# Sliding-window attention and a hardswish MLP on one core: batch 1 in 64x64 tiles, first-product units moved ahead of its steps, a token ring of six blocks

## Chip, core and metric

The kernel runs on one core of a Trainium2 chip. The metric is the device time of one execution in microseconds (us); less is better. The core has five engines that matter here, each with its own instruction queue: TensorE (PE, with its weight loads as PEld), VectorE (DVE), ScalarE (ACT), GpSimd (POOL) and SyncE (SP). DMA transfers are issued by SP and POOL and are carried out by 16 DMA engines.

## The reference

```python
def _attn_ref(q, k, v):                      # (8, 8, 576, 64) each
    scores = np.matmul(q, k.transpose(0, 1, 3, 2)) / np.sqrt(D)
    rel = pos[:, None] - pos[None, :]
    scores = np.where((rel >= 0) & (rel < 64), scores, -1e9)
    ... softmax over keys
    return np.matmul(attn, v)

def _moe_ref(x, w_in, w_out):                # x (4608, 512), w_in (512, 2048), w_out (2048, 512)
    h = x @ w_in
    g = h * np.clip(h + 3.0, 0.0, 6.0) / 6.0
    return g @ w_out
```

Attention runs over 8 batches of 8 heads, 576 positions and 64 dimensions; each query sees itself and the 63 keys before it. The heads of a token stand side by side in x, so x has 8 x 576 = 4608 rows of 512. The MLP takes x to 2048 and back to 512, with a hardswish between. Inputs and output are float32; the kernel's tiles are bf16.

## The kernel before

**Tiles and stages.** Attention goes in 32 steps t = 4b + g, one for each batch b and pair of heads g. The MLP goes in 9 blocks kb of 512 tokens. A block has 16 first-product units (`hT`, L467 to L471: four matmuls of 128x512 over the 512 rows of w_in), each followed by ACT's relu (L473) and DVE's min and multiply (L474) into `gT`, and 16 second-product units (`acc`, L491 to L495: four matmuls each), of which every fourth closes an output tile that ACT copies (L498) and SP stores (L500). x is kept transposed in `xT`, a ring of XR = 5 x 512 tokens (L57), which a step writes at the place of its batch modulo XR.

**Two forms of a step.** Batches 0 and 1 use the early form. q and k are loaded as 96 partitions of 6 rows (`load_early_qk`, L98), turned with 24 transposes (`t_k`, `t_q`, L221), and copied to `KT` by DVE (L239) and to `QZ` by ACT or DVE (L231). `s0_` (L244) adds the mask by a matmul of `ident` with `outside` ahead of each score matmul (L248, L251), 18 matmuls in all, so that exp (L259, L265) gives the masked weights at once. `pv_early` (L353) has 20 matmuls with the row sum as a 65th column, and `x_early` (L374) turns the result with 5 transposes on PE and a copy into `xT`.

Batches 2 to 7 use 64x64 tiles. q and k come in one tile of 2 x 64 partitions of 9 rows (`load_qk`, L117). `turn` (L276) makes 36 transposes into two PSUM banks, and `turned` (L283) copies them, keys by DVE and queries by ACT. `s_first` and `s_rest` (L296, L310) make 36 score matmuls without a mask, the first four into spare columns of the banks of `turn`. `weights` (L316) takes exp on ACT (L319, L322) and multiplies by the masks `first` and `band` on POOL (L327, L330). `pv` has 48 matmuls (L403). `pv_out` (L412 to L422) sums, inverts and multiplies on DVE, and `x_` (L429) sends the result into `xT` with DMA transposes on SP (L436): one for the big part (`opl`) and one for the first 64 tokens (`opg` in the profile), or four and one where the batch runs over the end of the ring.

V of a batch lies twice in memory: as loaded (`Vn`, or `Un` for 64x64 tiles) and shifted by 64 tokens (`Vs` or `Us`). The shifted copy is made by DVE and ACT for batch 0, and by two or more DMAs on SP otherwise (`shift_early` L149 and L150, `shift` L155 and L156). `Un` and `Us` need columns of ones beside the values (`pads`, L140 and L141). The tiles of batch b share the memory of batch b - 2.

**PSUM.** `ps_o` has one buffer of two banks, `ps_t` three of one, `ps_h` two and `ps_acc` one. A first-product unit of block 0 uses `ps_h`, and for fc 2, 5, 8 and 11 the buffer of `ps_o` (L462).

**Order.** There is no scheduler: each engine's queue has the order in which the program issues. `queue_block(kb)` (L509) puts the 16 first-product units of a block into `moe`, mixed evenly with what is left of the block before's second-product units, and `weave(n)` (L524) issues the next n. L619 to L649 load and set up, L652 to L680 run batch 0, L705 to L745 batch 1, between units of block 0. From t = 7 on `group(t, n)` (L682) issues pv(t), turn(t + 2), the scores of t + 1, pv_out(t), the key copy, x_(t), two units, the query copy and n - 2 units. From step 12 on a step has 8 units.

The loads of q, k, V and the weights are issued by POOL in program order (L620 to L640 for the start). In the start the queue holds batch 0, w_in in three parts, q and k of batch 1's first two pairs, its V in five pieces, q and k of its other two pairs, and w_out in two parts.

Of the kernel before, what the change touches and what calls it, by code (L numbers as in the profile page):

```python
# [20 lines left out]
BIG = 3.0e38  # L21
# [4 lines left out]
D = 64  # L26
# [10 lines left out]
def kernel(  # L37
# [19 lines left out]
    XR = 5 * TB  # L57
# [40 lines left out]
    def load_early_qk(b, pairs, first=0):  # L98
        if first:
            tiles = staged[b]  # L100
        else:
            both = stage.tile([SP, 2, H, R * D], BF16, name="qk6", tag="qk")
            tiles = [both[:, 0], both[:, 1]]
        h = 2 * first
        for n in pairs:
            for t, src in zip(tiles, (q, k)):
                nc.gpsimd.dma_start(  # L107
                    out=t[:, h : h + 2 * n, :],
                    in_=src[b, h : h + 2 * n].rearrange("h (p r) d -> p h (r d)", r=R),
# [4 lines left out]
    def load_qk(b):  # L114
        t = stage.tile([P, H, RL * D], BF16, name="qk9", tag="qk")
        for z, src in enumerate((k, q)):
            nc.gpsimd.dma_start(out=t[halves[z]], in_=src[b].rearrange("h (p r) d -> p h (r d)", r=RL))  # L117
        return t

    def load_early_v(b):  # L120
        vn = Vn[b % 2]
        for m in range(NM):
            n = min(P, S - m * P)
            nc.gpsimd.dma_start(  # L124
                out=vn[:n, m, :, 0:D],
                in_=v[b, :, m * P : m * P + n, :].rearrange("h s d -> s h d"),
# [11 lines left out]
    def pads(b):  # L138
        for t in (Un[b % 2], Us[b % 2]):
            nc.gpsimd.memset(t[:, :, :, 0:VO], 1.0)  # L140
            nc.gpsimd.memset(t[:, :, :, VO + P : VW], 1.0)  # L141

    def shift_early(b, blocks=(0, NM), heads=(0, H), move=nc.sync.dma_start):

        vn, vs = Vn[b % 2], Vs[b % 2]
        hs = slice(*heads)
        m0, m1 = blocks
        m2 = min(m1, NM - 1)
        move(out=vs[W:P, m0:m1, hs], in_=vn[0:W, m0:m1, hs])  # L149
        move(out=vs[0:W, m0 + 1 : m2 + 1, hs], in_=vn[W:P, m0:m2, hs])  # L150
# [32 lines left out]
    def window(t, inside, fill):  # L183

        nc.gpsimd.memset(t[:], inside)
        for sign, base in ((-1, -1), (1, W)):
            nc.gpsimd.affine_select(
                out=t[:], in_=t[:], pattern=[[sign, W]], compare_op=ISGE,
                fill=fill, base=base, channel_multiplier=-sign,
# [9 lines left out]
    def late_windows():  # L199

        for t in (band, first):
            nc.gpsimd.memset(t[:], 1.0)
# [24 lines left out]
    def t_q(t):  # L227
        b, g = divmod(t, NG)
        tp = transposed_heads(ps_t if b else ps_h, staged[b][0], g)
# [86 lines left out]
    def weights(t, s, ss):  # L316
# [3 lines left out]
        for h in range(2):  # L320
# [48 lines left out]
    def x_early(t):  # L369
# [7 lines left out]
        x0 = b * S % XR  # L377
        n = min(S, XR - x0)
        for to, i, j in ((x0, 0, n), (0, n, S)):
            if i < j:  # L380
# [414 lines left out]
```

## Time and profile before

| what | value |
|---|---|
| runs | 336.97, 334.5, 332.69 us; median 334.5 |
| profiled execution | 335.91 us, span 334.2 us |
| mean granted PE clock | 0.989 |
| PE busy | 312.8 us (94%), 4592 matmuls |
| ACT busy | 190.2 us (57%) |
| DVE busy | 173.7 us (52%) |
| POOL busy | 116.5 us (35%) |
| first products on PE (L468) | 143.9 us |
| second products on PE (L492) | 145.3 us |
| POOL's mask products (L330, L327) | 54.2 us and 15.9 us |
| HBM read, written | 36.70 MB, 9.44 MB |

The page gives the busy time of each engine, the span in 40 slices (a digit is the busy share in tenths; PEclk is the clock that PE was granted), the DMA queues, the chain of work that ended last, the costliest groups of instructions, and the DMA issues with their time to landing. Busy times of different engines overlap. The trace behind the page can be asked for the waits of an engine, for a timeline of it, in which square brackets give the idle time before an instruction and what ended it, and for the busy times of chosen stretches. In timelines several instructions of one line are drawn together (x24), with their starts and modelled ends, so neighbours overlap by their pipelining; the distance from start to start is what an instruction costs its engine.

### The profile page before, as it was taken

To read this page: it belongs to the slowest core of one execution; us is meant where nothing else is said; L and a number is where in the kernel's file an instruction comes from. 1 tells how busy PE (TensorE), PEld (TensorE's weight loads), DVE (VectorE), ACT (ScalarE), POOL (GpSimd) and SP (SyncE) were. 2 spreads that over 40 slices of the span, in tenths; PEclk is the share of its full clock that TensorE was granted. 3 is DMA by queue.
4 is the path that set the end of the run, shared out by engine and by line. 5 is a ranking of instruction groups with operands and counts; after the bars stand their busy time and mean duration, and the time that the engine had idled before them with its cause. 6 is when DMAs were issued, how large, how long until landed. Compare 5 with 4: busy or idle time off the path is not lost.

```text
span 334.2 us, 10639 instructions
## 1 busy us (share of the span) xinstructions
PE 312.8 (94%) x4592; PEld 160.4 (48%) x4592; DVE 173.7 (52%) x356; ACT 190.2 (57%) x345; POOL 116.5 (35%) x154
## 2 busy tenths in 40 slices
PE   6979599999799999999899999999999999999992
PEld 2744365454555555555455555555544444444440
DVE  7676357447655555555455555555554543334300
ACT  2868583457676666666566666666664444454320
POOL 8934612136566335633554356333330000000000
PEclk9999889999999999999999999999999999999997
DMA  6999999932339943993499329931111100001011
GB/s 89 165 210 179 231 209 192 199 93 62 92 74 193 118 113 60 187 113 111 79 175 124 115 55 189 121 113 55 52 51 49 65 31 31 33 31 64 32 68 69
DMA packets 59015, 35.86 MB, mean 107 GB/s; under 512 B 40528, under 2 KB 52880, under 8 KB 58960
## 3 DMA queue, kind: packets, MB, share of 16 engines
q0 software_dynamic: 36752, 18.35, 44.2%
q1 hardware_dynamic: 22208, 16.75, 19.5%
q8 instruction: 38, 0.62, 0.7%
q14 instruction: 17, 0.14, 0.1%
HBM read 36.70 MB, written 9.44 MB: 138 GB/s over the span
## 4 chain that ended last, share of the span: by engine, by line
PE 81%; DMA 8%; POOL 5%; ACT 2%; DVE 1%; SPq 1%; issue 1%; POOLq 0%; ACTq 0%
PE acc L492 36%; PE hT L468 34%; DMA qk<-in_q_dram 4%; PE o L403 3%; DMA qk<-in_k_dram 3%; PE s L310 2%; POOL qk L107 1%; PE tk L276 1%; POOL V L124 1%; DVE gT L474 1%; ACT t L473 1%; SPq L436 1%; DMA xT<-opg 1%; PE tq L276 1%; POOL Pz L330 1%
## 5 line engine op out<-in xcount | busy, mean ns | idle before, releaser
L474 DVE SCALAR_TENSOR_TENSOR gT<-t,hT 128x512 bf16<-128x512 bf16 x140 | 96.3, 688 | 126.9 <-ACT t L473 126.8
L473 ACT ACTIVATE t<-hT,half_const 128x512 bf16<-128x512 f32 x140 | 96.2, 687 | 93.0 <-PE hT L468 91.8
L468 PE MATMUL hT<-xT,win 128*128 128x512 bf16 x560 | 143.9, 381 | 4.6 <-DMA xT<-opg 1.7
L492 PE MATMUL acc<-wout,gT 128*128 128x512 bf16 x576 | 145.3, 379 | 0.2 <-DVE gT L474 0.2
L468 PEld LDWEIGHTS <-win 128*128 128x128 bf16 x576 | 55.8, 98 | 68.0 <-issue 3.7
L492 PEld LDWEIGHTS <-gT 128*128 128x128 bf16 x576 | 54.4, 98 | 65.1 <-issue 2.3
L330 POOL TENSOR_TENSOR Pz<-e,band 128x512 bf16<-128x512 bf16 x48 | 54.2, 1145 | 0.0
L327 POOL TENSOR_TENSOR P<-e,first 64x256 bf16<-64x256 bf16 x24 | 15.9, 661 | 103.5 <-ACT e L319 103.5
L498 ACT COPY osb<-acc 128x512 f32<-128x512 f32 x36 | 21.1, 585 | 21.3 <-PE acc L492 20.9
L322 ACT ACTIVATE e<-s 128x512 bf16<-128x512 f32 x48 | 25.7, 590 | 0.0
L283 DVE COPY KT<-tk 128x576 bf16<-128x576 bf16 x24 | 17.7, 739 | 0.6 <-PE tq L276 0.6
L422 DVE TENSOR_TENSOR opl<-o,recs 128x256 bf16<-128x256 f32 x48 | 17.7, 405 | 0.0
L403 PEld LDWEIGHTS <-Pz 64*64 64x64 bf16 x960 | 11.3, 108 | 10.4 <-issue 9.3
L283 ACT COPY QZ<-tq 128x576 bf16<-128x576 bf16 x24 | 15.2, 632 | 0.6 <-PE tq L276 0.6
L133 POOL DMA_DIRECT2D V<-in_v_dram x18 | 14.4, 815 | 0.0
L403 PE MATMUL o<-V,Pz 64*64 64x65 bf16 x960 | 14.1, 195 | 0.1
L231 ACT COPY QZ<-tp 64x576 bf16<-64x576 bf16 x12 | 7.6, 631 | 10.6 <-PE tp L221 10.6
L276 PE MATMUL tq<-ident,qk 64*64 64x64 bf16 x432 | 12.3, 195 | 0.5 <-DVE gT L474 0.5
L276 PE MATMUL tk<-ident,qk 64*64 64x64 bf16 x432 | 12.4, 195 | 0.0
L310 PE MATMUL s<-QZ,KT 64*64 64x64 bf16 x768 | 12.3, 195 | 0.0
L221 PE MATMUL tp<-ident,qk 96*64 96x96 bf16 x192 | 5.6, 208 | 6.0 <-DMA qk<-in_k_dram 6.0
L276 PEld LDWEIGHTS <-qk 64*64 64x64 bf16 x864 | 10.4, 105 | 1.5 <-issue 1.4
(84 smaller groups left out, 227.0 us busy)
## 6 DMA issues: line engine op xcount, KB each, us to landing
out_dram<-osb SPq DMA_DIRECT2D x36, 256.0 KB, 2.2
qk<-in_k_dram POOLq DMA_DIRECT2D x6, 576.0 KB, 6.4
qk<-in_q_dram POOLq DMA_DIRECT2D x6, 576.0 KB, 10.0
V<-in_v_dram POOLq DMA_DIRECT2D x12, 256.0 KB, 6.1
V<-V SPq DMA_DIRECT2D x6, 432.0 KB, 4.5
wout<-in_moe_w_out_dram POOLq DMA_DIRECT2D x2, 1024.0 KB, 17.3
V<-in_v_dram POOLq DMA_DIRECT2D x8, 128.0 KB, 10.2
win<-in_moe_w_in_dram POOLq DMA_DIRECT2D x2, 512.0 KB, 8.0
```

Of the source, the lines that this page charges most:

```text
L276: nc.tensor.transpose(out=hosts[t][z][halves[h], r * W : (r + 1) * W], in_=staged[b][halves[z], 2 * g + h, r * D : (r + 1) * D], identity= ...
L283: (nc.scalar.copy if z else nc.vector.tensor_copy)(out=(QZ[t % 4][:, 0] if z else KT[t % 4][:, W:]).rearrange("q (p r) -> q p r", r=RL), i ...
L310: nc.tensor.matmul(ss[h][halves[i], c, m, r], lhsT=keys(t, h, W * (w - 1), r), rhs=QZ[t % 4][halves[h], 0, w * W : (w + 1) * W], start=Tru ...
L322: nc.scalar.activation(out=e[:].rearrange("p c m r w -> p (c m r w)"), in_=ss[h][:].rearrange("p c m r w -> p (c m r w)"), func=EXP, scale ...
L330: nc.gpsimd.tensor_tensor(out=Pw[t % 4][:, h].rearrange("p c m r w -> p (c m) (r w)"), in0=e[:].rearrange("p c m r w -> p (c m) (r w)"), i ...
L403: nc.tensor.matmul(o[halves[c], i, c0 : c0 + D + 1], lhsT=p, rhs=vt[:, 2 * g + h, v0 : v0 + D + 1], start=(r == 0), stop=(r == 1), skip_gr ...
L422: nc.vector.tensor_tensor(out=opg[:, :, i], in0=ov[:, i, 2:6, 1 : D + 1].rearrange("p (m h) d -> p m h d", h=2), in1=rec[:, i, 2:6].rearra ...
L468: nc.tensor.matmul(hT, lhsT=win16[:, g, fc * P : (fc + 1) * P], rhs=xT[:, g, t0 : t0 + TB], start=(g == 0), stop=(g == NG - 1),)
L473: nc.scalar.activation(out=t1[:], in_=hT, func=RELU, bias=half_const[:], scale=1.0 / 6.0)
L474: nc.vector.scalar_tensor_tensor(out=gT[:, fc, :], in0=t1[:], scalar=1.0, in1=hT, op0=MIN, op1=MULT)
L492: nc.tensor.matmul(acc[:], lhsT=gT[:, fc, ts * P : (ts + 1) * P], rhs=wout16[:, fc, :], start=(fc == 0), stop=(fc == NFC - 1),)
L498: nc.scalar.copy(out=osb[:], in_=acc[:])
```

## The change

Batch 1 (t = 4 to 7) is done in the 64x64 form, and the code for the early form is cut to batch 0. The parts:

- The ring holds 6 blocks of 512 tokens. Then batch 5 (tokens 2880 to 3456) is the one that runs over its end, at 3072. `x_` now splits the big part into at most two transposes at a multiple of 128 tokens.
- q and k of batch 1 are loaded by `load_qk` in two halves of two pairs, its V by `load_v` in three pieces, and its shifted V by `shift(1)`, two DMAs on SP right behind the issues of V.
- The mask tiles are made at the start (`late_windows`), ahead of the loads of batch 1. The memsets of `ident`, `outside`, `band`, `first` and the pads of batch 1 go to DVE; that of `recs` goes later.
- In steps 5 to 7 two of the three mask products, `P0` and the one of the second head, go to DVE (`both`); step 4 has all three on POOL.
- x of steps 4 and 5 goes by DMA transposes, that of 6 and 7 by PE transposes and an ACT copy (`x_turned`).
- The first three units of block 0 are split: three of their four matmuls are issued ahead of `x_early(3)` and the fourth behind it (`begin`), in place of two warm-up matmuls.
- The order of steps 4 to 8 is written out anew, with more units of block 0 before each of them and fewer second-product units between; the order from pv(12) on is as before. The loads of batches 2 and 3 and the shifts of V move with it: q, k and V of batch 2 stand on POOL behind the mask products of step 7, those of batch 3 behind step 8's.
- The PSUM pools of block 0's units are dealt out anew (`ps_acc`, `ps_t` and `ps_o` for single units), and second products of block 0 use `ps_acc` alone.

```diff
-    XR = 5 * TB
+    XR = 6 * TB
...
-    def load_qk(b):
-        t = stage.tile([P, H, RL * D], BF16, name="qk9", tag="qk")
+    def load_qk(b, n=NG, first=0):
+        t = staged[b] if first else stage.tile([P, H, RL * D], BF16, name="qk9", tag="qk")
+        hs = slice(2 * first, 2 * (first + n))
...
-    def weights(t, s, ss):
+    def weights(t, s, ss, muls=(nc.gpsimd,) * 3):
...
-                nc.gpsimd.tensor_tensor(
+                muls[2].tensor_tensor(
                     out=P0[t % 4][:], in0=e0[:], in1=first[0:D].unsqueeze(1).to_broadcast([D, 2, 2, W]), op=MULT
...
-            nc.gpsimd.tensor_tensor(
+            muls[h].tensor_tensor(
                 out=Pw[t % 4][:, h].rearrange("p c m r w -> p (c m) (r w)"),
...
-        edge = (XR - W - x0 % XR) if x0 % XR < XR < x0 % XR + S else NM * P
-        m1 = min(edge // P, NM - 1)
+        m1 = min(NM - 1, (XR - W - x0 % XR) // P)
...
+        for i, j in ((0, m1), (m1, NM - 1)):
+            if i < j:
+                to_x(x0 + W + i * P, flat[:, i:j].rearrange("p m c -> p (m c)"), P, j - i)
...
+    def x_turned(t):
+        b, g = divmod(t, NG)
+        opg, opg0 = opgs.pop(t)
+        tp = ps_t.tile([P, S], BF16, name="xp", tag="bk")
+        nc.tensor.transpose(out=tp[:, 0:W], in_=opg0[:].rearrange("p h d -> p (h d)"), identity=ident[0:D, 0:D])
+        for m in range(NM - 1):
+            nc.tensor.transpose(
+                out=tp[:, W + m * P : W + (m + 1) * P],
+                in_=opg[:, m // 2, m % 2].rearrange("p h d -> p (h d)"), identity=ident[:],
+            )
+        nc.scalar.copy(out=xT[:, g, b * S : b * S + S], in_=tp[:])
...
-            if kb == 0 and fc % 3 == 2 and fc < spare[0]:
-                hT = ps_o.tile([P, 2, 512], F32, name="hTo", tag="o")[:, 0]
+            if part < 2 and fc in halfway:
+                hT = halfway.pop(fc)
             else:
-                pool = ps_t if late[0] == 1 or late[0] and fc % 2 else ps_h
+                if pool is None:
+                    if late[0] == 0:
+                        pool = (ps_h, ps_h, ps_o)[fc - 3] if fc < 6 else ps_t if fc % 2 else ps_acc
+                    else:
+                        pool = ps_t if late[0] == 1 or fc % 2 else ps_h
...
-            for g in range(NG):
+            for g in ((0, 1, 2), (3,), range(NG))[part]:
...
-                    pool = ps_t if (late[0] == 2 or kb == 0) and ts % 2 else ps_acc
+                    pool = ps_t if late[0] == 2 and ts % 2 else ps_acc
...
+    def begin(kb, pools, between):
+
+        for fc, pool in enumerate(pools):
+            moe.popleft()
+            units[kb](fc, 0, pool)
+        between()
+        for fc in range(len(pools)):
+            units[kb](fc, 1)
...
-    staged[1] = load_early_qk(1, pairs=(2,))
-    load_early_v(1)
-    load_early_qk(1, pairs=(NG - 2,), first=2)
+    late_windows()
+    staged[1] = load_qk(1, 2)
+    load_v(1)
+    shift(1)
+    load_qk(1, 2, 2)
...
-    warm(ps_acc, 2)
-    x_early(3)
-
+    queue_block(0)
+    begin(0, (ps_acc, ps_t, ps_t), lambda: x_early(3))
...
-    queue_block(0)
-    weave(6)
-    t_k(NG)
-    t_q(NG)
+    both = (nc.gpsimd, nc.vector, nc.vector)
+    n = NG
+    weave(4)
+    turn_two(n)
     weave(1)
-    for g in range(1, NG):
-        t_k(NG + g)
-        t_q(NG + g)
-        weave(1)
-        s0_(NG + g - 1)
-        weave(1)
-    shift_early(1, blocks=(0, 3))
-    shift_early(1, blocks=(3, NM))
+    turn_two(n + 1)
+    front(n, n + 1)
+    weave(1)
+    front(n + 1, n + 1, both)
+    weave(1)
+    pv(n)
+    pv_out(n)
+    x_(n)
+    weave(1)
+    turn_two(n + 2)
+    pv(n + 1)
+    pv_out(n + 1)
+    x_(n + 1)
+    weave(1)
+    turn_two(n + 3)
+    front(n + 2, n + 3, both)
+    weave(1)
+    front(n + 3, n + 3, both)
+    weave(1)
+    pads(2, nc.gpsimd.memset)
     staged[2] = load_qk(2)
-    pads(2)
     load_v(2)
+    pv(n + 2)
+    pv_out(n + 2)
+    weave(1)
+    pv(n + 3)
+    pv_out(n + 3)
+    x_turned(n + 2)
+    weave(len(moe))
+    late[0] = 1
+    queue_block(1)
+    weave(1)
+    x_turned(n + 3)
     shift(2)
-    late_windows()
+    weave(9)
+    turn_two(2 * NG)
+    weave(2)
+    group(2 * NG - 1, 2)
     staged[3] = load_qk(3)
...
+    pads(3, nc.gpsimd.memset)
     load_v(3)
```

`turn_two(t)` is `turn(t)` and both copies of `turned`; `front(t, host, muls)` is the scores and `weights` of step t.

More of the change, by code (lines that the diff above doesn't have):

```diff
@@ L95, with load_early_qk @@
     halves = (slice(0, D), slice(D, P))
-    def load_early_qk(b, pairs, first=0):
+    def load_early_qk(pairs, first=0):
         if first:
-            tiles = staged[b]
+            tiles = staged[0]
         else:
@@ L136, in load_v, with pads, shift_early @@
             )
-    def pads(b):
+    def pads(b, memset):
         for t in (Un[b % 2], Us[b % 2]):
[L140 to L150, printed above, removed]
+            memset(t[:, :, :, 0:VO], 1.0)
+            memset(t[:, :, :, VO + P : VW], 1.0)
+    def shift_early(g, move):
+        vn, vs = Vn[0], Vs[0]
+        hs = slice(2 * g, 2 * g + 2)
+        move(out=vs[W:P, :, hs], in_=vn[0:W, :, hs])
+        move(out=vs[0:W, 1:NM, hs], in_=vn[W:P, 0 : NM - 1, hs])
     def shift(b):
@@ L476, in unit @@
             )
+        units[kb] = unit
         return [lambda fc=fc: unit(fc) for fc in range(NFC)]
```

106 lines of the change are left out of this document (42 added, 64 removed).

## The prediction

> **What bounds the kernel now.** I read the page's busy line and slices first.
>
> ```profile
> PE 312.8 (94%) x4592; PEld 160.4 (48%) x4592; DVE 173.7 (52%) x356; ACT 190.2 (57%) x345; POOL 116.5 (35%) x154
> ...
> PE   6979599999799999999899999999999999999992
> ...
> PEclk9999889999999999999999999999999999999997
> DMA  6999999932339943993499329931111100001011
> ```
>
> TensorE bounds it nearly everywhere. A slice is 8.36 us: PE is short of 9 in slices 1, 3, 5 and 11 and a little in slice 20; its clock dips in slices 5 and 6, where the DMA engines are full. So only the first 93 us and one later place have anything but matmul work to lose. Next PE's waits, from 14 to 45 us and then from 100 us on:
>
> ```profile
> PE tp L221 <- DMA qk<-in_k_dram: 4.3, 2, 3.7
> ```
>
> ```profile
> PE hT L468 <- DMA xT<-opg: 1.7, 1, 1.7
> ```
>
> The first is the load of batch 1's q and k. The timeline of PE shows where it bites, and a wait of another kind, a VectorE one after the scores of step 9:
>
> ```profile
> 38.87 0.70 PE L221 MATMUL tp<-ident,qk 96*64 96x96 bf16 x24 [3.74 <-DMA qk<-in_k_dram]
> ...
> 69.56 0.81 PE L468 MATMUL hT<-xT,win 128*128 128x512 bf16 x3 [0.76 <-DVE gT L474]
> ```
>
> After the idle time comes a stretch at half clock (columns: PE, PEld, DVE, ACT, POOL busy, clock, DMA share, GB/s):
>
> ```profile
> 36.67:40.09 3.42, 1.22 (x27) 0.87 (x28) 1.07 (x2) 0.47 (x1) 2.28 (x9) 1.00 1.15 265
> 40.09:43.50 3.41, 3.41 (x24) 2.43 (x22) 0.72 (x2) 2.84 (x6) 0.00 (x0) 0.50 1.24 214
> ```
>
> A unit (4 matmuls of 128x512) takes .864 at full clock, so 3.41 us at .50 lose 1.7. The 1.66 us wait in slice 20 is block 4 waiting for the last x transpose; SyncE's timeline shows why:
>
> ```profile
> 155.28 5.57 SPq L436 DMA_TRANSPOSE xT<-opl  x4
> 160.89 1.82 SPq L436 DMA_TRANSPOSE xT<-opg  x1
> ...
> 163.44 1.24 SPq L436 DMA_TRANSPOSE xT<-opl  x1
> 164.73 1.21 SPq L436 DMA_TRANSPOSE xT<-opg  x1
> ```
>
> Batch 4 (tokens 2304 to 2880) runs over the ring's end at 2560: five transposes a step instead of two.
>
> **The stretch that changes** runs from 22.59 us (after x_early(2)) to 93.39 (the start of pv(12)): 70.8 us. Both orders have done 48 units by then, and what follows is the same except for the ring and one queue. PE's waits there are .37, .54, 3.74, .49 (turn 8), .76, .34, .19, .33, .79, .79, with 1.7 lost to the clock: 10.0 in all, so 60.8 is work.
>
> **Work removed.** An early step costs PE, by start to start in its timeline: 24 transposes .63, 18 score and mask matmuls 1.0, 20 pv matmuls .44, 5 transposes .28: 2.35. A step in 64x64 tiles costs 36 transposes .31, 36 score matmuls .42, 48 pv matmuls .41: 1.14. Four steps save 4.8; the turned x of steps 6 and 7 gives back 2 x .28 = .6, and two warm matmuls (.6) go: 4.8 net.
>
> **What the new order waits for first** is the shifted V of batch 1, which pv(4) needs. V's pieces keep their place behind q and k of the first two pairs and their bytes. These are the last V piece, issued at 22.03, and the last piece of the shift before, issued at 35.30 (columns: size, us to landing):
>
> ```profile
> V<-in_v_dram POOLq DMA_DIRECT2D x1, 64.0 KB, 12.7
> ```
>
> ```profile
> V<-V SPq DMA_DIRECT2D x1, 72.0 KB, 6.5
> ```
>
> So V lands at 34.7 and the shift at 41.8. Two early memsets leave POOL (.22 and .17, L621, L185): I take .3 off. The affine selects (1.9 us) move ahead of the batch 1 loads, at nothing: POOL idles there 4.42 for the DMA queue; without that cover +1.9. SyncE's two issues (.58, .59) now wait for V, with nothing queued behind them before x(4). So Us is there at 34.5 + 6.7 = 41.2. Bounds: the 432 KB shifts took 6.8 loaded (issued at 61.8) and 4.0 unloaded (84.6): 38.5 to 41.4. I take the loaded one: slices 4 and 5 are full.
>
> PE reaches pv(4) earlier. The split of the first three units costs 0: warm .6 and the .37 wait leave, xp moves behind three quarters, and unit 2 still ends near 26.8 because x of pair 2 needs its copy. Then three last quarters .65, seven units 6.05, turns 4 and 5 .62, scores 4 and 5 .84, changes of tile size .6 and short bank waits .9: 36.5. It idles 4.7 us, and the half clock follows: from 41.2 to 43.5, losing 1.15.
>
> The Trainium skill, "TensorE: Matmul & The Clock Gate", Part 1 (The HAM clock gate), says the clock falls after at least one idle window of about 3.4 us. The row above differs: 2.2 us idle in a window with 1.22 busy was enough. By the page a 4.7 us idle need not hold a whole window, and the sum would be 1.15 less.
>
> **From 41.2 to pv(12)**: 38 units 32.8; 8 turns 2.5; 7 scores 2.9; 8 pv 3.3; 2 x .3 turned x; 12 changes of tile size at .1: 43.3, so 84.5. To this come waits:
> - clock 1.15 (0 to 1.7).
> - Keys 6 and 7: between hT10 and scores 7 VectorE has two gT (.69), two K copies (.74) and a pv_out (1.35: L412 to L422 at 75.40 to 76.75): 4.2, behind ACT's t .69 and hand-offs: 5.4 to 5.7 against 3.2 of PE work: 2.5 (0 to 2.9).
> - pv(7) needs the one ps_o buffer back: gT and pv_out of 6, 2.0, against one unit: 1.2 (0 to 1.4).
> - pv(8) needs step 8's masks from POOL: 3.3 from scores to the last product at step 9 (68.8 to 72.1), against two units, 1.8: 1.5 (0 to 1.6).
> - pv(9): its masks queue on POOL behind qk 3 (2 x .70), pads (4 x .2) and V 3:
>
> ```profile
> 106.06 2.41 POOL L133 DMA_DIRECT2D V<-in_v_dram  x3
> ```
>
>  4.4 + 2.9 of products against 5.7 of PE: 1.6 (0 to 2.5).
> - Turned x of 7 .24, turn 9 .25, banks .9: 1.4 (.5 to 2).
>
> Together 9.35: pv(12) at 93.85 against 93.39: +.45. Six of the twelve mask products of batch 1 (three of 64x256, three of 128x512) move to VectorE behind the scores of steps 5 to 7, two a step. No row has them: the bounds are .30 (a copy of 64x576, L150) and POOL's .66 and 1.145; I take .4, as L422 (128x256, two inputs), and nothing on the path: they stand behind ACT's exponentials (.27, .26, .59, .59, L319 and L322), and pv comes a unit or more later.
>
> q, k and V of batch 2 are now issued behind POOL's product of step 7, by my sum at 52 to 53, where they went at 45 and 57 before. With .8 of pads ahead, .70 an issue and 9.5 to landing (the q load issued at 97 to 99) q is there at 63; turn 8 comes 16 units after pv(4)'s start, near 64: no wait, 0 to 2 if the cover of 1 us is gone. V 2 lands near 63 and its shift 4.0 later, before pv(8) near 69. The memsets given to VectorE (band, first, pads: about 1.3) run before 22 us while loads are awaited; uncovered they cost up to 1.3.
>
> **After pv(12).** x(11) stands on SyncE behind shift(3), which now waits for V 3 (issued late by POOL): block 2 waits +.7 (0 to 2). The ring of six blocks (3072) ends inside batch 5, which wraps with three transposes instead of five, 3.7 us a step: block 4's stall goes, -1.75 (1.66 plus the restart); next late is the ordinary 2.4 of two transposes, inside 8.17 us a step.
>
> Sum: +.45 + .7 - 1.75 = -.6. The profiled execution took 335.91 (span 334.2), 1.4 above the median of 334.5; 335.9 - .6 - 1.4 = 333.9 for the median.
>
> **The rivals.**
> A, the forecast: work saved 4.8 and the old waits (10) are paid back by an equal set of new ones: 333.9, alone 331.5 to 336.5. Chance .47.
>
> B, the shift lands as if unloaded, by 38.5: idle 2 instead of 4.7, no clock loss: -2.7 - 1.15: 330.0. For: SyncE's queue is not POOL's, and wout's 2 MB are issued after it. Against: all four shift pieces of before took 6.5 to 6.7 in this place. Chance .2; with the waits at pv(7) to pv(9) also at their low ends (-4.3) it is 325.7, a third of it.
>
> C, slower: the shift takes its time by bytes. Before it went in pieces of 216 and 72 KB at 6.5 to 6.7; as 432 KB behind a full queue it could take twice 6.7: Us at 48, PE idle 11.5, a second half-clock window: +6.8 + 1.7: 342.4. From Us at about 42 it ends slower than before, from 46.8 by over 2%. Against: 432 KB took 6.8 at 61.8. Chance .1.
>
> D, VectorE's products are dear: at POOL's prices the six take 5.4 instead of 2.4, in the chain that already ends last at keys 7 and pv(7): +3.0: 336.9. Against: VectorE's two-input rows run at .405 for 256 columns. Chance .13. The Trainium skill, "GPSIMD Engine Reference", section 1 (Specifications), says that GpSimd shares its SBUF interfaces with VectorE and contends with VectorE instructions of two SBUF inputs, which these are; no run of before has the pair.
>
> E, the ring does not do what it says: three transposes a step still let SyncE fall behind and the wait moves to block 5: +1.75: 335.7. Against: 3.7 in 8.17 leaves room where 7.4 did not. Chance .1.
>
> **How the numbers follow.** 2% is 6.7 us, about what a measurement of this kernel can tell from no change. Under 327.8: a third of B and the tail of A's low waits, .1. Over 341.2: C and a tail of D, .12. Between: .78. The range 329.0 to 339.0 holds A, two thirds of B, D and E, and leaves out C and B's low end. Predicted: 333.9.
>
> **What would show it.** Right: pv(4) waits 4 to 5 us for V<-V and starts near 41; one window at .50 follows; scores 7 wait for KT, pv(8) and pv(9) for POOL; pv(12) starts at 93 to 95; no wait for xT in block 4. Wrong: pv(4) before 39 or after 43; VectorE products over .7; waits behind pv(4) under 5 us in all; hT of block 2 waiting over 2 us for xT.

## The result and the profile after

The changed kernel takes 336.56 us (median of 20 runs, 334.96 to 338.35) where the kernel before takes 334.62 us (20 runs, 332.4 to 338.35): 1.0066 of its time, 95% interval 1.004 to 1.0092. It is slower by about 2 us. The forecast was 333.9, a little faster. The profiled execution of the changed kernel took 338.35 us, the longest of the 20 runs, with a span of 336.6 us; no other of the 20 has a lower mean granted clock than its 0.974, and the highest is 0.998. So what is read from this trace on the clock is the upper end of what the change costs there.

The page of the changed kernel, the lines that answer to those shown first:

```profile
PE 308.8 (92%) x4770; PEld 157.8 (47%) x4812; DVE 175.9 (52%) x376; ACT 188.8 (56%) x347; POOL 120.4 (36%) x154
...
PE   6987367988999999999999999999999999999992
...
PEclk9799878999999999999999999999999999999997
DMA  7999992939937932993299429941111110001011
```

PE is busy 4 us less: work went away as meant. But slices 4 to 7 (a slice is 8.4 us), where PE had 9, 5, 9, 9 before, now have 7, 3, 6, 7, and the clock dips in slices 5 to 7 and in slice 2. The dip in slice 2 left no delay that can be seen: pv(3) starts at 21.75 us, before at 21.70. The slice of the old block 4 stall (20) is full. So the loss lies in front of 60 us and the gain behind 93 us. PE's waits from 22 to 100 us:

```profile
PE o L393 <- DMA V<-V: 4.0, 1, 4.0
PE tk L292 <- DVE KT L279: 3.5, 2, 2.1
PE o L393 <- POOL Pz L326: 2.6, 4, 0.9
PE o L393 <- DVE opl L412: 1.9, 1, 1.9
PE hT L472 <- ACT xT L373: 1.0, 2, 0.7
```

They stand in order of size: the shifted V ahead of pv(4), the copies of keys ahead of scores 4 and 6, POOL's mask products ahead of pv(8) and pv(9), and the results of step 6 ahead of pv(7). The three longest in the timeline of PE (lines of three narrow stretches):

```profile
41.56 0.91 PE L393 MATMUL o<-V,Pz 64*64 64x65 bf16 x30 [4.04 <-DMA V<-V]
...
49.63 0.20 PE L292 MATMUL tk<-QZ,KT 64*64 64x64 bf16 x1 [2.12 <-DVE KT L279]
...
57.36 0.45 PE L393 MATMUL o<-V,Pz 64*64 64x65 bf16 x32 [1.93 <-DVE opl L412]
```

The stretch from 22.6 us to the start of pv(12), first in the kernel before, then in the changed kernel (PE, PEld, DVE, ACT, POOL busy, clock, DMA share, GB/s):

```profile
22.60:93.39 70.79, 62.35 (x1058) 34.71 (x1056) 39.82 (x76) 44.19 (x83) 28.26 (x46) 0.98 1.04 158
```

```profile
22.60:98.22 75.62, 59.57 (x1265) 31.22 (x1277) 42.32 (x90) 43.11 (x85) 31.69 (x42) 0.93 1.01 150
```

With half of the busy time at clock .50 counted as loss, the 70.8 us before are 60.6 of work, 8.4 idle and 1.7 lost to the clock; the 75.6 us after are 55.8 of work, 16.1 idle and 3.7 lost to the clock. The work saved is 4.8. Idle time grew by 7.6 and the clock's loss by 2.0. (The page after has 4770 matmuls beside 4812 weight loads, so some matmul records are missing, and idle time is rather too high than too low.) From the start of pv(12) to the end of the span it is 240.8 before and 238.4 after. So: +4.8 up to pv(12), -2.4 behind it, +2.4 in the span.

### The profile page after: what moved, and what is told of

It reads as the page before. It is cut to its first block, busy times and chain, and to the rows that moved or that the text cites. A ratio compares the mean times of both kernels' runs of the same rounds, so it can differ in the third digit from the quotient of the medians.

```text
span 336.6 us, 11066 instructions
## 1 busy us (share of the span) xinstructions
PE 308.8 (92%) x4770; PEld 157.8 (47%) x4812; DVE 175.9 (52%) x376; ACT 188.8 (56%) x347; POOL 120.4 (36%) x154
## 4 chain that ended last, share of the span: by engine, by line
PE 78%; DMA 7%; POOL 7%; DVE 2%; issue 2%; ACT 2%; SPq 0%; POOLq 0%; ACTq 0%
PE acc L500 36%; PE hT L472 33%; DMA V<-in_v_dram 5%; PE o L393 4%; PE s L306 2%; DMA V<-V 2%; PE tk L272 1%; POOL qk L107 1%; POOL V L126 1%; POOL Pz L326 1%; ACT t L480 1%; PE tq L272 1%; DVE gT L481 1%; POOL V L134 1%; POOL win L160 1%
## 5 line engine op out<-in xcount | busy, mean ns | idle before, releaser
L472 PE MATMUL hT<-xT,win 128*128 128x512 bf16 x561 | 147.3, 382 | 2.3 <-ACT xT L373 1.0
L472 PEld LDWEIGHTS <-win 128*128 128x128 bf16 x576 | 55.8, 99 | 67.6 <-issue 3.0
L500 PEld LDWEIGHTS <-gT 128*128 128x128 bf16 x576 | 54.2, 98 | 63.2 <-issue 0.6
L326 POOL TENSOR_TENSOR Pz<-e,band 128x512 bf16<-128x512 bf16 x53 | 60.2, 1154 | 13.6 <-ACT e L318 13.6
L318 ACT ACTIVATE e<-s 128x512 bf16<-128x512 f32 x56 | 30.0, 588 | 0.7 <-PE s L306 0.7
L393 PE MATMUL o<-V,Pz 64*64 64x65 bf16 x1120 | 17.6, 198 | 8.7 <-DMA V<-V 4.0
L393 PEld LDWEIGHTS <-Pz 64*64 64x64 bf16 x1120 | 14.0, 111 | 20.7 <-issue 15.6
L279 DVE COPY KT<-tk 128x576 bf16<-128x576 bf16 x28 | 20.7, 740 | 0.0
L412 DVE TENSOR_TENSOR opl<-o,recs 128x256 bf16<-128x256 f32 x56 | 20.6, 405 | 0.0
L279 ACT COPY QZ<-tq 128x576 bf16<-128x576 bf16 x28 | 17.7, 633 | 0.4 <-PE tq L272 0.4
L315 ACT ACTIVATE e<-tk 64x128 bf16<-64x128 f32 x28 | 7.5, 270 | 12.3 <-PE tq L292 12.3
L306 PEld LDWEIGHTS <-KT 64*64 64x64 bf16 x896 | 11.3, 110 | 0.7 <-issue 0.7
```

Source lines behind the costliest of these rows:

```text
L279: (nc.scalar.copy if z else nc.vector.tensor_copy)(out=(QZ[t % 4][:, 0] if z else KT[t % 4][:, W:]).rearrange("q (p r) -> q p r", r=RL), i ...
L306: nc.tensor.matmul(ss[h][halves[i], c, m, r], lhsT=keys(t, h, W * (w - 1), r), rhs=QZ[t % 4][halves[h], 0, w * W : (w + 1) * W], start=Tru ...
L318: nc.scalar.activation(out=e[:].rearrange("p c m r w -> p (c m r w)"), in_=ss[h][:].rearrange("p c m r w -> p (c m r w)"), func=EXP, scale ...
L326: muls[h].tensor_tensor(out=Pw[t % 4][:, h].rearrange("p c m r w -> p (c m) (r w)"), in0=e[:].rearrange("p c m r w -> p (c m) (r w)"), in1 ...
L393: nc.tensor.matmul(o[halves[c], i, c0 : c0 + D + 1], lhsT=p, rhs=vt[:, 2 * g + h, v0 : v0 + D + 1], start=(r == 0), stop=(r == 1), skip_gr ...
L412: nc.vector.tensor_tensor(out=opg[:, :, i], in0=ov[:, i, 2:6, 1 : D + 1].rearrange("p (m h) d -> p m h d", h=2), in1=rec[:, i, 2:6].rearra ...
```

## The experiments

A measure that all runs share is the time from the start of pv(3), the last of batch 0, to the start of pv(12), and from there to the end of the span. It is read from each run's one profiled execution; the ratio to the kernel before, with its 95% interval, is from the timed runs.

| run | pv(3) to pv(12), us | pv(12) to end, us | ratio to the kernel before |
|---|---|---|---|
| before | 71.7 | 240.8 | 1 |
| changed | 76.5 | 238.4 | 1.0066 (1.004 to 1.0092) |
| e1 ring alone, old form | 68.5 | 243.0 | 0.9947 (0.9911 to 0.9984) |
| e5 ring and split of x, old form | 68.2 | 238.3 | 0.988 (0.9819 to 0.9942) |
| e15 the same again | 68.1 | 238.6 | 0.992 (0.9881 to 0.9959) |
| e2 no wait for the shift | 74.5 | 238.4 | 1.0002 (0.997 to 1.0034) |
| e3 zeros ahead of pv(4) | 74.6 | 238.4 | 1.0057 (1.0019 to 1.0095) |
| e4 scores first | 75.4 | 238.4 | 1.0041 (1.0005 to 1.0078) |
| e6 scores ahead of pv(4) | 80.4 | 238.4 | 1.0226 (1.0165 to 1.0287) |
| e7 loads of batch 3 early | 77.0 | 238.9 | 1.0055 (1.0008 to 1.0103) |
| e8 e6, e7 and DVE products | 76.9 | 238.5 | 1.0099 (1.0059 to 1.0139) |
| e9 changed again | 76.4 | 238.4 | 1.0041 (1.0006 to 1.0075) |
| e10 zeros in three waits | 74.4 | 239.2 | 1.0061 (1.0023 to 1.0098) |
| e11 e6 with four buffers | 77.3 | 238.5 | 1.0144 (1.0105 to 1.0182) |
| e12 all masks on POOL | 75.3 | 238.5 | 1.0014 (0.9976 to 1.0051) |
| e13 units in the wait | 74.8 | 239.7 | 1.0087 (1.0048 to 1.0126) |
| e14 V first | 74.8 | 239.1 | 1.0085 (1.0047 to 1.0123) |
| e16 second units in steps 5 to 7 | 78.5 | 239.5 | 1.011 (1.0055 to 1.0165) |
| e17 e16 and small edits | 74.3 | 239.0 | 1.0078 (1.0048 to 1.0107) |

Two theories were tested. The first: the loss is the wait for the shifted V and the half clock behind it. The rival: steps 4 to 11 in the new form give ScalarE, VectorE and POOL more to do one after the other than the units between can cover, and a wait taken away comes back at the next step.

### The ring

e1 changes one line of the kernel before.

```diff
-    XR = 5 * TB
+    XR = 6 * TB
```

> The kernel before with the ring of six blocks and nothing else. The ring theory: block 4 no longer waits 1.66 us for the x transposes, nothing else moves: 1.8 to 2.2 us under the kernel before, about 332.6 us. The rival, three transposes a step in batch 5 make SyncE fall behind instead: a wait for xT of about 1.7 us in block 5, and the time of the kernel before.

The rival's outcome came true, by five transposes a step and not by three: the old `x_` splits the big part into four. Block 4 no longer waits, but a wait of the same kind stands behind batch 5. The waits of PE from 100 us on, and SyncE's transposes in batch 5:

```profile
PE hT L468 <- DMA xT<-opg: 2.1, 1, 2.1
```

```profile
183.70 6.73 SPq L436 DMA_TRANSPOSE xT<-opl  x4
190.47 2.13 SPq L436 DMA_TRANSPOSE xT<-opg  x1
```

From pv(12) to the end it takes 2.2 us more than before: the wait is .4 longer, and behind it the clock is at half from 194.1 to 197.5 us, which loses 1.7. Its timed runs are still 0.5% faster. The part ahead of pv(12), which has the code of before, took 68.5 instead of 71.7 in this execution (why, stands below); whether that also sets the timed runs apart is not shown. e5 adds the changed `x_`:

```diff
-        edge = (XR - W - x0 % XR) if x0 % XR < XR < x0 % XR + S else NM * P
-        m1 = min(edge // P, NM - 1)
+        m1 = min(NM - 1, (XR - W - x0 % XR) // P)
...
+        for i, j in ((0, m1), (m1, NM - 1)):
+            if i < j:
+                to_x(x0 + W + i * P, flat[:, i:j].rearrange("p m c -> p (m c)"), P, j - i)
```

> The kernel before with the ring of six blocks and the changed x_, which splits the big part at a multiple of 128 tokens, so that batch 5 has three transposes a step where the ring alone had five. Theory: no wait for xT in block 4 or 5, 1.7 to 2.1 us off the span from pv(12) to the end against the kernel before: about 333 us beside 335. Rival, three transposes still put SyncE behind: a wait for xT in block 5 again, as with the ring alone (2.1 us).

> The kernel before with the ring of six blocks and the changed x_ once more, in one job with the others, for a narrower interval. Expected .985 to .995 of the kernel before, that is 1.7 to 5 us less; about 2.2 us by the trace from pv(12) on, the rest being how early q and k of batch 1 landed in the runs at hand.

The theory held: no wait for xT from 100 us on, and 2.2 to 2.5 us less from pv(12) to the end, as in the changed kernel, whose timeline of SyncE shows the three transposes of a step in batch 5:

```profile
182.74 2.83 SPq L426 DMA_TRANSPOSE xT<-opl  x2
185.62 1.22 SPq L426 DMA_TRANSPOSE xT<-opg  x1
```

So the ring needs the split: six blocks alone only move the stall, and both together remove it. This is the one part of the change that gains, and without the rest it beats both kernels: 0.988 and 0.992 of the kernel before, 331.45 and 331.7 us.

e1, e5 and e15 have the old form up to pv(12), and their three executions show what the recorded one of before did not: q and k of batch 1's last pairs cost 1.4 to 1.8 us instead of 3.7, and the clock did not dip ahead of pv(12). PE's line in e5 beside the one shown of before, and the stretch in e5:

```profile
36.72 0.70 PE L221 MATMUL tp<-ident,qk 96*64 96x96 bf16 x24 [1.80 <-DMA qk<-in_k_dram]
```

```profile
22.60:89.66 67.06, 60.45 (x1056) 33.48 (x1054) 39.54 (x76) 43.85 (x83) 28.16 (x46) 1.00 1.05 167
```

That is 60.4 of work, 6.6 idle and nothing lost to the clock. Against these, the two recorded executions of the changed kernel take 8 us more from pv(3) to pv(12), not 4.8. That is too much for a typical run: the recorded executions of e5 and e15 are among their fastest (329.7 and 330.24 us), those of the changed kernel among its slowest. By the timed runs the rest of the change costs 1.5 to 1.9% (1.0066 against 0.992 and 0.988), 5 to 6 us.

### The wait for the shifted V

e2 lets pv of batch 1 read the V that is not shifted (that part of its result is another one):

```diff
-                            p, vt = Pw[t % 4][halves[i], h, c, m, r], (Us if c else Un)[b % 2][halves[i], m]
+                            p, vt = Pw[t % 4][halves[i], h, c, m, r], (Us if c and b != 1 else Un)[b % 2][halves[i], m]
```

> The changed kernel, but pv of steps 4 to 7 reads V unshifted where it should read the shifted copy, so that part of the result of batch 1 is another one; the shift itself is still made, and nobody in batch 1 waits for it. Theory that the wait for the shifted V (4.0 us) and the half clock behind it (about 1.9) are what the change lost: pv(4) starts its last matmuls by 38, pv(12) at 92 to 93 instead of 98.2, time 330.5 to 331.5 us. Rival, the waits between the steps behind it (keys, buffers, masks) take the time back: pv(12) after 96, time 334.5 us or more.

Between the two, nearer the rival: pv(5) starts at 40.43 instead of 44.94, pv(12) at 96.29 instead of 98.22. Of 4 us, 1.9 were left at pv(12), and by the timed runs e2 (1.0002) is .6% under the changed kernel's 1.0066, but not clearly under the 1.0041 of its second measurement, e9. The waits of PE from 22 to 100 us show where the others went:

```profile
PE o L393 <- POOL Pz L326: 3.3, 5, 0.9
PE tk L292 <- DVE KT L279: 2.5, 2, 1.5
PE o L393 <- DVE opl L412: 1.7, 2, 1.0
PE o L393 <- issue: 1.5, 1, 1.5
PE s L306 <- DVE recs L404: 1.4, 1, 1.4
```

A wait of scores 6 for VectorE and one inside pv(5) are new, and the clock was at .50 from 42.7 to 52.9 us, with no wait over 1.6 us in front. That loses 4.1 us, as much as the changed kernel loses to its clock.

e3 and e10 put idle matmuls into the waits, 16 ahead of pv(4) in e3, and 9 and 7 more ahead of scores 6 and pv(7) in e10:

```diff
     weave(1)
+    warm(ps_acc, 16)
     pv(n)
...
     turn_two(n + 3)
+    warm(ps_t, 9)
     front(n + 2, n + 3, both)
...
     weave(1)
+    warm(ps_t, 7)
     pv(n + 3)
```

> The changed kernel with 16 matmuls on zeros (3.5 us at full clock) ahead of pv(4), where TensorE otherwise waits. It does no useful work more; it only keeps TensorE busy. Theory that the half clock after the wait costs its share: no window at .5 or .6 from 40 to 47 us, 1 to 2 us less than the changed kernel: 334.5 to 335.5 us. Rival, the chain over ScalarE and VectorE sets the steps behind pv(4), and the clock of TensorE doesn't: 336.5 us. Should the second dip at 50 to 54 us stay, the gain is 1 us at most.

> The changed kernel with matmuls on zeros in its three longest waits: 16 ahead of pv(4), 9 ahead of scores 6, 7 ahead of pv(7). They compute nothing. Theory that the half clock costs about 3 us from pv(4) to pv(12): no window under .9 from 36 to 60 us, and pv(12) 52.5 to 53.5 us after the shifted V instead of 56.4. Rival, the waits are set by ScalarE, VectorE and DMA and lengthen by what the matmuls gain: pv(12) 55 us or more after the shifted V.

In e3 the first dip went and the second stayed (48.1 to 51.5 us); from the start of pv(4)'s matmuls to pv(12) it took 55.6 us, against 56.7 in the changed kernel. In e10 no dip was left behind pv(4), and the same stretch took 54.2 us. So in this stretch the clock is worth 1 to 2.5 us. But neither kernel is faster than the changed one by its runs, though the mean granted clocks of e10's twelve runs lie between .989 and .998. In its recorded execution the clock fell before, from 34.1 to 37.5, the 16 matmuls then lasted to 41.0, and pv(4) started later than V allowed (SyncE's second issue at 32.81 and 6.5 to landing: 39.3).

The runs of the changed kernel themselves say how far the clock accounts for the loss. Of the twelve of e9, four have a mean clock of .991 or more, with a median of 335.5 us; the eighteen such runs of the kernel before that were taken beside them have 333.6. These are few runs, but with the clock equally high on both sides about the same 2 us are left. So the clock is not the whole loss, and the idle time has a part in it.

e14 issues V and its shift ahead of q and k, puts four more units ahead of turn 4 and replaces them later by second-product units of block 0:

```diff
-    staged[1] = load_qk(1, 2)
     load_v(1)
     shift(1)
+    staged[1] = load_qk(1, 2)
...
-    weave(4)
+    weave(8)
     turn_two(n)
...
+    moe.extend(left[:5])
+    del left[:5]
```

> The changed kernel with V of batch 1 and its shift issued ahead of q and k of the first two pairs, and with four more units ahead of turn 4 in exchange, filled up later with five second-product units of block 0. Theory: V lands near 29 and the shift by 36, q and k of pairs 0 and 1 by 33, so that turn 4 waits under 1 us and pv(4) not at all: pv(4) near 39, no half clock, pv(12) 4 to 6 us earlier than 97.3: 331 to 333 us. Rival, as with no wait for the shift at all (96.3), the steps behind it give back most: 335 us.

The rival held. SyncE issued the shift at 29.65, no wait for it and no dip ahead of pv(7) are left, and pv(12) started at 96.63, with a dip from 82.5 to 85.9 among the new waits. Waits that were 2.6 and 1.9 in the changed kernel are longer:

```profile
PE o L393 <- POOL Pz L326: 4.6, 6, 1.4
PE o L393 <- DVE opl L412: 2.9, 2, 1.6
PE tk L292 <- DVE KT L279: 2.7, 2, 1.8
```

e13 keeps the loads and puts the four units into the wait, ahead of pv(4):

```diff
     front(n + 1, n + 1, both)
-    weave(1)
+    weave(5)
     pv(n)
```

> The changed kernel with four more first-product units ahead of pv(4), in the wait for the shifted V, and five second-product units of block 0 in their old places, so that every place before pv(7) has as many units as before. The work is the same in all; the steps from 8 on have four units fewer between them. Theory that the wait and the clock are what is lost: no half clock from 37 to 47, pv(7) at the same time as in the changed kernel or up to 2 us earlier, and pv(12) 3 to 5 us earlier than 97.3: 332 to 334 us. Rival, the steps from 8 on take it back, since POOL's mask products and the buffers of pv are then less covered: pv(12) at 96 or later, 336 us.

The rival again: the clock did not fall behind pv(4), but already from 35.9 to 39.3 among the units ahead of it, pv(4) came at 44.2, later than V, and the waits for POOL grew to 3.9 in all, up to 1.4, with a dip from 83.7 to 87.1. The theory that the wait for V and the clock behind it are the whole loss has fallen: the wait, removed in three ways, brought .5 to 1.9 us at pv(12), and e14, which has neither the wait nor a dip before 82 us, brought 1.6.

### The steps behind

e4 issues scores 4 and 6 ahead of the copies of steps 5 and 7, whose banks they share:

```diff
-    turn_two(n + 3)
-    front(n + 2, n + 3, both)
+    turn(n + 3)
+    s = s_first(n + 2, n + 3)
+    ss = s_rest(n + 2)
+    turned(n + 3, 0)
+    turned(n + 3, 1)
+    weights(n + 2, s, ss, both)
```

> The changed kernel, in which the scores of steps 4 and 6 are issued ahead of the copies of the keys and queries of steps 5 and 7, whose banks they share, as the later steps do it. Theory that the 2.1 us wait of scores 6 for the key copy of step 7 is a wait on the bank alone and lies on the path, with a half-clock window behind it: scores 6 start at 47.5 instead of 49.6, no dip at 50 to 54, pv(12) 2 to 3 us earlier: 333.5 to 334.5 us. Rival, the copy of the keys of step 7 is late in any case and the wait moves to scores 7 and pv(7): 336 us or more.

Inconclusive by the runs (1.0041, against 1.0066 and 1.0041 of the changed kernel): pv(6) started 3.9 us earlier, at 50.03, pv(7) 3.2 and pv(12) 1.1 us earlier. But 2.1 of that are V, which let pv(4) go on at 39.50 instead of 41.56; counted from there, pv(12) came .9 later. The wait of 2.1 for keys went. The one for the results of step 6 stayed (2.1), waits of 1.2 for VectorE's reciprocals and .8 for exponentials came, and a half clock from 55.4 to 58.8.

e6 puts turns and scores of steps 6 and 7 ahead of pv(4):

```diff
     front(n + 1, n + 1, both)
     weave(1)
+    turn_two(n + 2)
+    weave(1)
+    front(n + 2, n + 2, both)
+    turn_two(n + 3)
+    weave(1)
+    front(n + 3, n + 3, both)
     pv(n)
```

> The changed kernel with the turns and scores of steps 6 and 7, and two units, ahead of pv(4), so that they fill the wait for the shifted V; the units behind it are fewer by two. Theory that the steps behind pv(4) have too little TensorE work between to cover the copies of keys and queries, and that this and the half clock cost about 8 us from pv(4) to pv(7): pv(4) still ends near 42.5, but pv(7) starts by 51 instead of 57.4 and pv(12) at 93 to 95 instead of 98.2: 332 to 333.5 us. Rival, the load of the other two pairs of q and k (landed at 38) or the two banks of the turns hold step 6 up, so that pv(4) starts later by as much: pv(12) after 97, 336 us.

Worse than either theory had it: 342.78 us. A wait that nobody had in mind, in the timeline of VectorE:

```profile
58.31 0.28 DVE L407 TENSOR_TENSOR opg<-o,recs 64x128 bf16<-64x128 f32 x1 [7.13 <-DMA xT<-opg]
```

The result of step 6 goes into the buffer of step 4's, of which there are two, and step 4's has to be read by its DMA transposes first. POOL was through with the masks early, so it issued the loads of batch 2 at 46 to 50 us, and the transposes of the same time landed late: 8.6 to 9.8 us after their issue, where those of steps 4 and 5 in the changed kernel took 4.1 to 5.1 without these loads (issues from 46 to 53 us; size, us to landing):

```profile
V<-in_v_dram POOLq DMA_DIRECT2D x2, 256.0 KB, 12.6
...
xT<-opl SPq DMA_TRANSPOSE x2, 9.8
xT<-opg SPq DMA_TRANSPOSE x2, 8.6
```

e11 gives these results four buffers:

```diff
-        opg = work.tile([P, 2, 2, 2, D], BF16, name="opl")
+        opg = oplp.tile([P, 2, 2, 2, D], BF16, name="opl")
```

> The kernel with the scores of steps 6 and 7 ahead of pv(4), with four buffers instead of two for the results of pv (opl, opg0), so that pv_out of step 6 needn't wait until the x transposes of step 4 have landed. Theory: the 7.1 us wait of VectorE and the 6.9 us of pv(7) go, pv(7) starts at 52 to 53 instead of 59.4 and pv(12) at 95 to 97: 333.5 to 336 us. Rival: the transposes are late for block 1 as well, whose first unit then waits for xT: no better than 340 us.

pv(7) starts at 52.32, as expected, but then block 1 waits 3.4 us for xT, from the same late transposes: pv(12) at 99.03. Theory and rival both held, one after the other.

e7 moves the issues of batch 3's loads to where POOL idles, right behind pv(7):

```diff
     x_turned(n + 3)
     shift(2)
+    staged[3] = load_qk(3)
+    pads(3, nc.gpsimd.memset)
+    load_v(3)
     weave(9)
```

> The changed kernel with the issues of q, k and V of batch 3 and their pads right behind pv(7), while POOL idles, instead of behind the mask products of step 8. Theory that these 4.4 us on POOL are what pv(9) waits for: pv(9) starts with 0.3 us of wait or less instead of 1.5, shift(3) lands earlier, pv(12) 1 to 1.5 us earlier: 335 to 335.5 us. Rival, pv(9) is held by the products themselves (2.9 us after the scores): no difference.

Neither held. pv(9) no longer waits for POOL (0.5 in all from 2.6), but the early loads run beside the shift of batch 2, and pv(8) waits for that. The first wait of PE from 22 to 100 us, where the changed kernel had 4.0 once:

```profile
PE o L393 <- DMA V<-V: 6.5, 3, 2.8
```

e8 adds this to e6 and puts all mask products of steps 5 to 7 on VectorE:

```diff
-    both = (nc.gpsimd, nc.vector, nc.vector)
+    both = (nc.vector, nc.vector, nc.vector)
```

> The two edits before together, and all mask products of steps 5 to 7 on VectorE. Theory: the gains of the scores ahead and of the early loads add up (4 to 6 us), and VectorE's products take .28 and .41 us each, as they did where POOL had none at the time, instead of .92 and 1.0 beside one of POOL's: pv(12) at 91 to 93, 330 to 332 us. Rival, VectorE's chain gets longer by the products that POOL had (0.41 each) and the waits for key copies and buffers grow by as much: no better than the scores ahead with the early loads by themselves.

It kept e6's wait for the transposes (7.3 us at pv(7)), so it says little of the masks but their price: .28 (in steps 6 and 7) and .42 with none of POOL's beside them, where theory had .28 and .41. e12 goes the other way, all on POOL:

```diff
-    both = (nc.gpsimd, nc.vector, nc.vector)
+    both = (nc.gpsimd,) * 3
```

> The changed kernel with all mask products on POOL, as in the kernel before. Theory that those on VectorE cost as they stand (.28 to .92 and .41 to 1.0 us) no more than POOL's: pv(6) and pv(7) come later by the two products that POOL has to do more (1.8 us a step, some 1 to 2 us at pv(12)): 337.5 to 338.5 us. Rival, VectorE's products lie in the chain of key copies and results, and taking them out shortens it: 335.5 us.

Its 1.0014 lies below the 1.0041 of e9, but the intervals overlap: unclear. From pv(4) going on (40.36) to pv(12) it took 56.7 us, as in the changed kernel. It was not the loss that was expected; moving products to VectorE brought no gain that these runs show.

e9 is the changed kernel once more.

> The changed kernel once more, for a second profiled execution: the last piece of V of batch 1 landed at 34.7 in the first and at 32.3 to 34.0 in its variants. Expected if the wait for the shifted V is what decides: with V at 32.5 pv(4) and all behind it come 2 us earlier, span 334.5. If the steps behind take it back: pv(12) within 1 us of 98.2 though V is early.

V was 1.6 us earlier (SyncE's first issue at 33.20 instead of 34.81) and pv(12) 0.9. But pv(3) was .9 earlier too (20.88 instead of 21.75): counted from there, V was .7 earlier and pv(12) .1. So the steps behind took it back, though .7 us is little to decide by.

e16 moves five second-product units of block 0 into steps 5 to 7; a helper `cover` takes them off `left`:

```diff
     turn_two(n + 3)
+    cover(2)
     front(n + 2, n + 3, both)
...
     front(n + 3, n + 3, both)
     weave(1)
+    cover(1)
...
-    weave(1)
+    weave(2)
     pv(n + 3)
...
     weave(len(moe))
+    cover(2)
```

> The changed kernel with five second-product units of block 0 taken out of the later steps: two where scores 6 wait for keys (2.1 us), one ahead of pv(6), two behind pv(7), whose place one more first-product unit takes. Useful work where TensorE idled 4 us; the wait for the shifted V stays. Theory that the steps behind pv(4) have too little work between them and that this alone is the loss: idle time from 22.6 to pv(12) falls from 16 to 12 to 13 us, the second half-clock window goes, pv(12) at 94 to 95: 333.5 to 334.5 us. Rival, as with units ahead of pv(4): steps 8 to 11, left with five units less, wait for POOL's products instead, idle stays at 14 to 16: pv(12) at 96 to 97, 336 us.

e17 adds e4's and e12's edits.

> The same with scores 4 and 6 ahead of the copies of steps 5 and 7, and all mask products on POOL. Theory: the waits for key copies (3.3 us) and VectorE's products beside POOL's (.92 and 1.0 instead of .28 and .41) go: 2 us less than the second units alone. Rival, masks become the last thing that pv(5) to pv(7) wait for, and nothing is gained.

e16 had V late in its execution (SyncE's first issue at 35.65), and its idle time stayed at 15.3: the rival. e17 has no wait for key copies over .6 left and 12.7 us idle where the changed kernel has 16.1, and still loses 3.0 to the clock; by its runs it is no better than the changed kernel. Its waits for POOL grew to 4.0.

**What stands.** The old form needs 68.1 to 71.7 us from pv(3) to pv(12) in four executions, the new one 74.3 to 80.4 in fifteen, whichever wait was removed. The new form's loss is thus shown, and it is not any one wait; the timed runs put it at 5 to 6 us. That the longer run of copies, exponentials, mask products and results of steps 4 to 11 sets the pace is argued from where the waits reappear (VectorE's copies and results, POOL's products), not shown by an experiment that shortens the whole of it. That stays open.

## Why the prediction was wrong, point by point

- **Work removed**, 4.8 forecast: 60.6 less 55.8 is 4.8. Right.
- **The shifted V**, 41.2 forecast: pv(4) got on at 41.56. Right for the recorded execution, though the landing differs by execution: SyncE's first issue of the shift, which waits for V, fell between 32.1 and 35.65 us in kernels with this order of loads.
- **Keys 6 and 7**, 2.5 forecast: 2.12 ahead of scores 6 and .34 behind them. Right in size, but it was the bank of step 7, not the key copy needed by scores 7: with the order of e4 it went.
- **pv(8), pv(9)**, 1.5 and 1.6 forecast: 1.3 and 1.3 (.46 and .85, .45 and .84). Right. **pv(7)**, 1.2 forecast: 1.93.
- **The clock**, "losing 1.15" in the sum: this step failed. In the recorded execution the loss is 3.7. The forecast laid the old kernel's one window over the new wait; in the trace the clock is at half from 39.43 to 46.26 us and from 49.67 to 53.09, three stretches of 3.41 us. The changed kernel, cut where its clock changes:

```profile
36.02:39.43 3.41, 1.50 (x42) 0.68 (x37) 2.54 (x4) 2.57 (x7) 3.41 (x3) 1.00 1.24 239
39.43:42.84 3.41, 1.20 (x47) 0.95 (x47) 0.10 (x1) 0.00 (x0) 0.21 (x1) 0.50 1.19 245
42.84:46.26 3.42, 3.20 (x88) 1.78 (x89) 1.89 (x7) 1.22 (x2) 0.00 (x0) 0.50 1.29 198
46.26:49.67 3.41, 1.22 (x44) 0.63 (x45) 3.25 (x9) 1.22 (x2) 0.00 (x0) 1.00 1.13 56
49.67:53.09 3.42, 3.08 (x76) 1.74 (x77) 1.36 (x3) 2.32 (x7) 1.16 (x1) 0.50 0.57 40
```

 The wait (37.5 to 41.56) lies in the first two stretches; PE is busy for 1.50 and 1.20 us of them, and the stretch behind each is at half clock. Behind the one with 3.20 busy the clock is back. The fourth, 1.22 busy around the wait of scores 6, is followed by half clock again, which the forecast had at nothing. The second recorded execution, e9, has two dips of the same lengths (38.18 to 45.01 and 48.42 to 51.83). The Trainium skill, "TensorE: Matmul & The Clock Gate", Part 1 (The HAM clock gate), has the full clock come back after a busy window of about 3.4 us, with which 42.84 to 46.26 agrees, and the fall after an idle one, from which 46.26 to 49.67 differs: 1.22 busy did not keep it up. In the timed runs the clock is only a part of the miss, since with an equally high clock about 2 us are left (above, with e10); the second step that failed stands below.
- **The sum from 41.2 to pv(12)**: 52.65 forecast, of which 43.3 work, 8.2 waits and 1.15 clock. Measured from 41.56:

```profile
41.56:98.22 56.66, 47.75 (x1073) 25.45 (x1084) 32.45 (x73) 31.64 (x63) 25.39 (x35) 0.93 0.89 129
```

 That is 56.7: 44.0 work, 8.9 idle and 3.7 clock. Of the 4.0 missing, 2.6 are the clock, .7 waits (pv(7) alone is .7 over) and .7 work. So the waits behind pv(4) were sized nearly right, and the clock was the term that was not.
- **The waits that go**, 10 us, were those of one execution: the second step that failed. In three others of the same old code they were 6.6 to 7.9 with no loss to the clock, and the wait for q and k was 1.4 to 1.8. The forecast took the wait of 3.74 and the dip behind it as the old form's own, so from pv(3) to pv(12) its base was 3.2 to 3.6 us slower than these three.
- **After pv(12)**: the ring was forecast at -1.75 and x(11) at +.7. It is -2.4 in all; no wait for xT in block 2 or later. Direction right, x(11) wrong, and 1.35 better than the -1.05 of the sum, which hides part of the miss before.

The forecast that new waits pay back the old ones was right in kind; they pay back more. A small gain was forecast and a loss came: up to pv(12) the recorded executions differ by +4.8 where the sum had +.45.

The rivals: B (V without a wait) did not come about, since V was there at 41.56 and not by 38.5, and its price is refuted, since e2 and e14 got 1.9 and 1.6 us where it had 3.85. C is refuted too: Us at 41.56, not at 48. E is refuted for the change as it stands; five transposes, in e1, did what it feared of three. D had a real mechanism, below: the six products on VectorE took 3.9 us, between the 2.4 of the forecast and the 5.4 of D, and of the signs of being wrong that were named, products over .7 came true. Its 336.9 lies next to the measured 336.56, but that is luck as far as is known: e12 takes the products off VectorE, and shows no gain that its interval clears.

## What to carry to other kernels

Before work is taken off the engine that bounds a stage, count what the stage's steps give the other engines one after the other: shorter steps on TensorE need more units between them, and a wait removed in such a chain mostly returned at the next step here. Take the price of a wait and of a clock dip from several executions, and a wait of some us as a risk for two windows at half clock. When parts of a change can stand alone, price and try them alone: here the ring with the split of x gains 0.8 to 1.2% and the rest loses more than that.

## What was not expected of the hardware

VectorE's and POOL's mask products hold each other up. The products of step 5 and 6 on VectorE, and POOL's of the same times, in the changed kernel's timelines:

```profile
37.37 0.92 DVE L323 TENSOR_TENSOR P<-e,first 64x256 bf16<-64x256 bf16 x1
38.22 0.41 DVE L326 TENSOR_TENSOR Pz<-e,band 128x512 bf16<-128x512 bf16 x1
...
50.44 0.28 DVE L323 TENSOR_TENSOR P<-e,first 64x256 bf16<-64x256 bf16 x1 [0.86 <-ACT e L315]
51.55 0.99 DVE L326 TENSOR_TENSOR Pz<-e,band 128x512 bf16<-128x512 bf16 x1 [0.82 <-ACT e L318]
```

```profile
38.11 1.53 POOL L326 TENSOR_TENSOR Pz<-e,band 128x512 bf16<-128x512 bf16 x1
```

```profile
51.11 1.16 POOL L326 TENSOR_TENSOR Pz<-e,band 128x512 bf16<-128x512 bf16 x1 [11.47 <-ACT e L318]
```

Alone the two take .28 and .41 on VectorE. Begun during one of POOL's products, VectorE's ends .27 us behind it (52.54 beside 52.27) and so lasts .99; where VectorE's ran as POOL's began, POOL's took 1.53 instead of 1.15. The Trainium skill, "GPSIMD Engine Reference", section 1 (Specifications), has GpSimd contend with VectorE instructions of two SBUF inputs; the traces agree. And DMA transposes, 2.4 to 2.6 us to landing in the steady part, took 8.6 to 9.8 in e6 beside loads of 1.7 MB: which transfers a faster engine sets off earlier decides who waits.
